# Expert 1's second weights issued behind the last attention step, and two late gathers side by side

## The chip, the cores and the metric

The kernel runs on one core of a Trainium2 chip. The metric is the device time of one execution in microseconds (us); the time before is the median of three runs.

## The reference

Attention over blocks of 64 positions for 8 batches of 8 heads (576 positions, 64 wide) gives 4608 rows of 512 numbers. A block of queries sees its own block of keys and all earlier ones. Each row is then sent to one of 8 experts, which its `domain_id` names:

```python
scores = np.where(mask, scale * q @ k.transpose(0, 1, 3, 2), -1e9)   # mask: block_i >= block_j
attn = softmax(scores); x = (attn @ v)                                # -> 4608 rows of 512
for e in range(8):
    rows = domain_id == e
    h = np.maximum(x[rows] @ w1[e], 0.0)      # w1[e]: 512 x 1024
    out[rows] = h @ w2[e]                     # w2[e]: 1024 x 512
```

The routing depends on `domain_id` alone. Each expert gets 640 slots (5 blocks of 128 rows); a loop at the end would serve an expert with more rows.

## The kernel before, in words

**Attention** runs in 33 steps (the loop at L535). Step p computes the scores of head pair p and the output of pair p - 1; a batch is four steps. The finished rows go to `x_rows`, a buffer in DRAM, by stores on SP's queue (`store_x`, L445): once per batch, and for the last batch in two pieces, 320 columns wide behind pair 30 and 192 columns wide behind pair 31. Each piece is two transfers (L448, L451).

**Experts.** For an expert the rows are gathered from `x_rows` into a tile `xg`, 128 rows at a time, transposed to `xT`, multiplied by w1 into `hT` (`mm1`, L650), by w2 into `po` (`mm2`, L663), and scattered to the output (L670). `xg` has four buffers, `xT` three. VectorE transposes a whole tile with 16 instructions (`turn`, L633); single blocks are transposed on TensorE and copied by VectorE (L482, L485).

The slots of each expert are filled so that its blocks 0 to 2 hold rows of batches 0 to 4 only. So these three blocks can be gathered while attention still runs on the last batches (`early_gather`, L499, which reads a shortened `x_rows`), and experts 0 and 1 begin with 384 columns each. Their blocks 3 and 4, and those of the others, need the last batch too: these gathers (`gather`, L468) wait for the last store. TensorE then goes through expert 0 blocks 0 to 2, expert 1 blocks 0 to 2, expert 0 blocks 3 and 4, expert 1 blocks 3 and 4, and after that experts 2 to 7 whole.

**What sets the order.** The schedule is written by hand: each engine executes what the program lists for it in that order. All loads of weights, all gathers and all scatters are issued by GpSimd (POOL) and go to one software DMA queue, q0; the stores of x go to SP's queue, q1. Both run on the same 16 DMA engines. POOL rotates over eight DMA semaphores (DMASW0 to DMASW7); before it issues a transfer it waits for the one that used the same semaphore eight transfers earlier.

Weights come in halves of 512 KB each: `load_weights` (L133) returns four functions, two halves of w1 and two of w2, and a list `todo` holds those still to be issued. The table `issue` (L528) says for each step what POOL issues behind it: a pair (e, w) is the early gather of expert e's block w, a 0 is the next half in `todo`. Behind the last step stand the remaining early gathers and then the late ones (L694 to L702).

Of the kernel before, what the change touches and what calls it, by code (L numbers as in the profile page):

```python
# [17 lines left out]
def kernel(  # L18
# [16 lines left out]
    NB = 5  # L35
# [5 lines left out]
    NE = 3  # L41
# [91 lines left out]
    def load_weights(w1_e, w2_e, pool=wsb, bufs=NW):  # L133
        w1h = pool.tile([128, 4, Fdim], F16, name="w1h", tag="w1h", bufs=bufs)
        w2h = pool.tile([128, 8, DM], F16, name="w2h", tag="w2h", bufs=bufs)
        return w1h, w2h, [lambda i=i: w1_half(w1h, w1_e, i) for i in range(2)] + [
            lambda i=i: w2_half(w2h, w2_e, i) for i in range(2)]
# [318 lines left out]
    def weights(e):  # L456
        where = (msb, 1) if e % (NW + 1) == NW else (wsb, NW)
        w1s[e], w2s[e], todo = load_weights(moe_w1[e], moe_w2[e], *where)
        return todo
# [6 lines left out]
    def gather(g, tok, blks):  # L466
        for blk in blks:
            nc.gpsimd.indirect_dma_start(  # L468
                out=g[:, blk, :], out_offset=None, in_=xd,
                in_offset=bass.IndirectOffsetOnAxis(  # L470
                    ap=tok[:, 1, blk : blk + 1], axis=0),
                bounds_check=N - 1, oob_is_err=False)

    def new_xg():
        return gsb.tile([128, NB, DM], F16, name="xg", tag="xg", bufs=4)

    def new_xT():
        return gsb.tile([128, 4, CAP], F16, name="xT", tag="xT", bufs=3)
# [18 lines left out]
    def early_gather(e, w):  # L497
        row = rows[e, w]
        nc.gpsimd.indirect_dma_start(  # L499
            out=xgs[e][:, w, :], out_offset=None, in_=xd[0 : N - LB * S],  # L500
            in_offset=bass.IndirectOffsetOnAxis(ap=row[:, 0:1], axis=0),
            bounds_check=N - LB * S - 1, oob_is_err=False)
# [17 lines left out]
    def turn_qk(*at):  # L520
        if at in Ts:
            G, s = Ts[at]
            if s == 0 and G > 1:
# [2 lines left out]

    prev = None
    issue = {22: (0, 0), 24: ((0, 0), 0), 25: ((0, 1), 0), 26: ((0, 2), 0),  # L528
             27: ((1, 0), 0), 28: ((1, 1), 0), 29: ((1, 2), 0), 30: ((2, 0),),
             31: ((2, 1),)}  # L530

    def tok_of(e):
        return tok0[:, :, NB * e : NB * e + NB]

    for p in range(npair + 1):  # L535
# [58 lines left out]
        if p == 22:  # L594
            todo = weights(0)
        if p == 24:
            todo += weights(1)
            xgs = [new_xg() for _ in range(4)]
# [42 lines left out]
    def new_hT():  # L641
        return msb.tile([128, 8, CAP], F16, name="hT", tag="hT", bufs=2)
# [49 lines left out]
        return outs[NB * e : NB * e + NB]  # L692

    early_gather(2, 2)  # L694
    for w in range(NE):
        early_gather(3, w)
    todo = weights(2)
    for e in range(3):
        for blk in range(NE, NB):
            gather(xgs[e], tok_of(e), (blk,))  # L700
            if e < 2 and blk == NE:
                todo.pop(0)()  # L702
    hT0, xT0, xT1, xT2 = new_hT(), xT, new_xT(), new_xT()
    turn(xgs[1], xT1, 0, NE)
    mm1(xT0, hT0, w1s[0], ((0, CE),))
# [2 lines left out]
    todo = weights(3)  # L708
# [28 lines left out]
    with tc.For_i(0, n_it, 1) as it:  # L737
# [5 lines left out]
        for _ in inv_high(msb, iv, NB, base_f[:, 0:1]):  # L743
# [7 lines left out]
        w1h, w2h, todo = load_weights(  # L751
            moe_w1[bass.ds(e_r, 1)].rearrange("o d f -> (o d) f"),
            moe_w2[bass.ds(e_r, 1)].rearrange("o d f -> (o d) f"))
# [38 lines left out]
```

## Time and profile before

| | us |
|---|---|
| median of 3 runs | 276.4 (272.78 to 277.53) |
| the profiled execution's own time | 274.43 |
| its span | 272.7 |
| TensorE busy (PE) | 252.2 (92%) |
| VectorE busy (DVE) | 186.8 (68%) |
| GpSimd busy (POOL) | 161.2 (59%) |
| mean granted TensorE clock | 0.975 |

Times in the rows below count from the start of the span. A wait in brackets is idle time of that engine just before the instruction, with what ended it. A POOL row of a transfer lasts as long as POOL writes its descriptors, not as long as the data move; the time from issue to landing is in the rows of the DMA view. An engine that is not busy costs nothing unless another waits for it.

### The profile page before, as it was taken

Reading aid. Unit: us, or ns where it says so; the run is one execution under the profiler, and the core shown is the slowest. Engines: PE = TensorE matmul, PEld = TensorE weight load, DVE = VectorE, ACT = ScalarE, POOL = GpSimd, SP = SyncE. Lnnn points to the kernel's source line nnn. Section 1 sums busy time; section 2 is a strip of 40 time slices with the busy share of each in tenths; the row PEclk is TensorE's granted clock in tenths of the full one; section 3 lists DMA queues with packets and bytes.
Section 4 is the critical chain, followed back from the end, with each engine's and each line's share of the span. In section 5 each row is a group of like instructions: output and inputs, shape, how many; then the busy total and the mean of one; then the engine's idle time right before and its main releaser. Section 6 shows DMA issues by size and latency. Waiting matters only on the chain.

```text
span 272.7 us, 7015 instructions
## 1 busy us (share of the span) xinstructions
PE 252.2 (92%) x2911; PEld 158.6 (58%) x2911; DVE 186.8 (68%) x303; ACT 164.9 (60%) x218; POOL 161.2 (59%) x189
## 2 busy tenths in 40 slices
PE   8999679999999999998799999999999999999940
PEld 5666456666666766663455665574655746647410
DVE  4589667999999787449149999079695893960000
ACT  1658667999999799953435655463553635536410
POOL 8798844644527156662888685477877876151240
PEclk9999977999999999999999999999999999999995
DMA  6999999999999999994889999999899996121130
GB/s 85 155 185 111 183 194 191 220 182 235 185 216 206 192 236 240 254 258 136 176 177 258 205 260 239 267 202 216 217 215 293 175 240 237 68 113 57 41 137 0
DMA packets 65665, 50.85 MB, mean 186 GB/s; under 512 B 41053, under 2 KB 53853, under 8 KB 65632
## 3 DMA queue, kind: packets, MB, share of 16 engines
q0 software_dynamic: 60016, 45.63, 98.0%
q1 hardware_dynamic: 5616, 4.76, 6.3%
q8 instruction: 24, 0.39, 0.5%
q14 instruction: 9, 0.07, 0.1%
HBM read 67.15 MB, written 15.20 MB: 302 GB/s over the span
## 4 chain that ended last, share of the span: by engine, by line
PE 57%; DMA 14%; issue 12%; POOL 10%; ACT 1%; POOLq 1%; DVE 0%; SPq 0%; ACTq 0%
PE ph L650 15%; PE po L663 14%; DMA kh<-in_k_dram 9%; PE ps L373 8%; PE po L415 8%; PE PT L362 6%; POOL out_dram L670 5%; PE po L426 4%; DMA xg<-x_rows,tok 4%; POOL vS L94 2%; DMA x_rows<-x 2%; PE ps L395 1%; POOL xg L468 1%; POOL qh L75 1%; ACT A L378 1%
## 5 line engine op out<-in xcount | busy, mean ns | idle before, releaser
L633 DVE STREAM_TRANSPOSE xT<-xg 32x640 f16<-32x640 f16 (+1 forms) x112 | 89.4, 798 | 22.8 <-DMA xg<-x_rows,tok 18.4
L378 ACT ACTIVATE A<-ps 128x1024 f16<-128x1024 f32 x96 | 92.0, 1024 | 16.7 <-PE ps L373 7.8
L650 PE MATMUL ph<-xT,w1h 128*128 128x320 f16 (+2 forms) x512 | 72.7, 299 | 3.1 <-DVE xT L633 2.8
L663 PE MATMUL po<-w2h,hT 128*128 128x512 f16 x320 | 71.0, 379 | 0.0
L654 ACT ACTIVATE hT<-ph 128x640 f16<-128x640 f32 (+2 forms) x80 | 47.8, 598 | 28.4 <-PE ph L650 26.3
L650 PEld LDWEIGHTS <-w1h 128*128 128x128 f16 x512 | 49.8, 98 | 25.9 <-issue 5.9
L670 POOL DMA_INDIRECT out_dram<-osb,tok x40 | 40.5, 1012 | 35.4 <-ACT osb L669 23.4
L663 PEld LDWEIGHTS <-hT 128*128 128x128 f16 x320 | 31.2, 98 | 35.5
L669 ACT COPY osb<-po 128x512 f32<-128x512 f32 x40 | 23.5, 586 | 46.6 <-PE po L663 42.1
L94 POOL DMA_DIRECT2D vS<-in_v_dram x45 | 36.2, 826 | 16.4 <-DMA kh<-in_k_dram 12.7
L365 DVE COPY QK<-PT 128x1152 f16<-128x1152 f16 x30 | 40.5, 1350 | 5.5 <-PE PT L362 5.5
L373 PE MATMUL ps<-QK 64*128 64x64 f16 (+3 forms) x320 | 40.2, 302 | 0.7 <-ACT A L378 0.6
L468 POOL DMA_INDIRECT xg<-x_rows,tok x28 | 28.4, 1014 | 15.6 <-issue 11.8
L415 PE MATMUL po<-vS,A 128*128 128x65 f16 x640 | 30.1, 198 | 0.4 <-DVE tf L225 0.3
L415 PEld LDWEIGHTS <-A 128*128 128x128 f16 x640 | 23.9, 100 | 9.7 <-issue 6.3
L439 DVE TENSOR_TENSOR x<-po,rc 128x640 f16<-128x640 f32 x32 | 26.4, 825 | 1.1
L499 POOL DMA_INDIRECT xg<-x_rows,row x12 | 12.6, 1048 | 15.5 <-DVE row L495 13.9
L426 PE MATMUL po<-vS,A 64*64 64x65 f16 (+1 forms) x320 | 21.2, 196 | 0.0
L373 PEld LDWEIGHTS <-QK 64*128 64x128 f16 x320 | 13.2, 95 | 6.1 <-issue 1.8
L426 PEld LDWEIGHTS <-A 64*64 64x64 f16 (+1 forms) x320 | 14.6, 108 | 1.9
L123 POOL DMA_DIRECT2D w1h<-in_moe_w_dram x16 | 12.2, 766 | 4.7 <-DMA qh<-in_q_dram 3.0
L438 DVE RECIPROCAL rc<-po 128x10 f32<-128x10 f32 x32 | 7.0, 220 | 10.5 <-PE po L426 9.7
(103 smaller groups left out, 142.4 us busy)
## 6 DMA issues: line engine op xcount, KB each, us to landing
w1h<-in_moe_w_dram POOLq DMA_DIRECT2D x16, 512.0 KB, 9.0
w2h<-in_moe_w_dram POOLq DMA_DIRECT2D x16, 512.0 KB, 9.5
x_rows<-x SPq DMA_DIRECT2D x7, 512.0 KB, 10.1
qh<-in_q_dram POOLq DMA_DIRECT2D x6, 576.0 KB, 13.1
kh<-in_k_dram POOLq DMA_DIRECT2D x6, 576.0 KB, 14.0
vS<-in_v_dram POOLq DMA_DIRECT2D x24, 128.0 KB, 11.8
vS<-in_v_dram POOLq DMA_DIRECT2D x23, 64.0 KB, 5.7
qh<-in_q_dram POOLq DMA_DIRECT2D x3, 288.0 KB, 6.7
```

The source lines that it names most:

```text
L94: nc.gpsimd.dma_start(out=vS[b % RV][r0:128, c, h0:h1, 16:80], in_=v[b, h0:h1, 128 * c : 128 * c + n, :].rearrange("h p d -> p h d"))
L365: nc.vector.tensor_copy(out=QKs[G][:, s].rearrange("p i (n j) -> p i n j", j=R), in_=P16.rearrange("p (j i n) -> p i n j", j=R, i=2))
L373: nc.tensor.matmul(out=o[:, t], lhsT=QK[h, 1, i, 128 * c : 128 * c + 128], rhs=QK[h, 0, i, q0:q1], start=True, stop=True)
L378: nc.scalar.activation(out=o, in_=i, func=AF.Exp, scale=0.125)
L415: nc.tensor.matmul(out=po[:, t, 65 * w : 65 * w + 65], lhsT=st["A"][:, t, n0 : n0 + 128], rhs=vS[b % RV][:, c, head(st, t), 15:80], start= ...
L426: nc.tensor.matmul(out=po[r0:128, t, 65 * w : 65 * w + 65], lhsT=st["A"][k : k + 64, t, n0 : n0 + 128 - r0], rhs=vS[b % RV][k : k + 64, c, ...
L468: nc.gpsimd.indirect_dma_start(out=g[:, blk, :], out_offset=None, in_=xd, in_offset=bass.IndirectOffsetOnAxis(ap=tok[:, 1, blk : blk + 1], ...
L633: nc.vector.transpose(out=dst[32 * j : 32 * j + 32, i, b0:b1], in_=src[32 * i : 32 * i + 32, j, b0:b1])
L650: nc.tensor.matmul(out=ph[:, i, 0:w], lhsT=w1_cols(w1h, dc, fc), rhs=xT[:, dc, c0 : c0 + w], start=(dc == 0), stop=(dc == 3))
L654: nc.scalar.activation(out=hT[:, fc, n0 : n0 + k * w].rearrange("p (i n) -> p i n", i=k), in_=ph[:, 0:k, 0:w], func=AF.Relu)
L663: nc.tensor.matmul(out=po[:], lhsT=hT[:, fc, 128 * blk : 128 * blk + 128], rhs=w2h[:, fc, :], start=(fc == 0), stop=(fc == 7))
L670: nc.gpsimd.indirect_dma_start(out=dst[blk], out_offset=bass.IndirectOffsetOnAxis(ap=tok[:, 0, blk : blk + 1], axis=0), in_=osb[:], in_off ...
```

## The change

The two halves of expert 1's w2 are no longer issued in steps 28 and 29 but behind the last step, after the gather of expert 3's block 0. Of the late gathers, the two of expert 0 now stand next to each other, as do those of expert 1 and of expert 2, with a half of expert 2's w1 between the pairs.

```diff
     issue = {22: (0, 0), 24: ((0, 0), 0), 25: ((0, 1), 0), 26: ((0, 2), 0),
-             27: ((1, 0), 0), 28: ((1, 1), 0), 29: ((1, 2), 0), 30: ((2, 0),),
+             27: ((1, 0), 0), 28: ((1, 1),), 29: ((1, 2),), 30: ((2, 0),),
              31: ((2, 1),)}
...
     early_gather(2, 2)
-    for w in range(NE):
+    early_gather(3, 0)
+    for f in todo:
+        f()
+    for w in range(1, NE):
         early_gather(3, w)
     todo = weights(2)
     for e in range(3):
-        for blk in range(NE, NB):
-            gather(xgs[e], tok_of(e), (blk,))
-            if e < 2 and blk == NE:
-                todo.pop(0)()
+        gather(xgs[e], tok_of(e), range(NE, NB))
+        if e < 2:
+            todo.pop(0)()
```

POOL from step 28 to the last early gather, before. `xg_2230` to `xg_2233` are the gathered rows of experts 0 to 3, `row11` is expert 1's block 1, `w2h_2229` is expert 1's w2:

```order
L499 DMA xg_2231<-x_rows,row11_2548 128x512 [waits DMASW1_49,DVE_49]
L128 DMA w2h_2229<-in_moe_w2_dram 128x2x1024 [waits DMASW2_49]
L499 DMA xg_2231<-x_rows,row12_2611 128x512 [waits DMASW3_49,DVE_49]
L128 DMA w2h_2229<-in_moe_w2_dram 128x2x1024 [waits DMASW4_49]
L499 DMA xg_2232<-x_rows,row20_2677 128x512 [waits DMASW5_49,DVE_49]
L499 DMA xg_2232<-x_rows,row21_2754 128x512 [waits DMASW6_49,DVE_49]
L499 DMA xg_2232<-x_rows,row22_2746 128x512 [waits DMASW7_49]
L499 DMA xg_2233<-x_rows,row30_2748 128x512 [waits DMASW0_49]
L499 DMA xg_2233<-x_rows,row31_2750 128x512 [waits DMASW1_49]
L499 DMA xg_2233<-x_rows,row32_2752 128x512 [waits DMASW2_49]
```

The same place in the changed kernel:

```order
L499 DMA xg_2231<-x_rows,row11_2548 128x512 [waits DMASW1_49,DVE_49]
L499 DMA xg_2231<-x_rows,row12_2610 128x512 [waits DMASW2_49,DVE_49]
L499 DMA xg_2232<-x_rows,row20_2675 128x512 [waits DMASW3_49,DVE_49]
L499 DMA xg_2232<-x_rows,row21_2752 128x512 [waits DMASW4_49,DVE_49]
L499 DMA xg_2232<-x_rows,row22_2744 128x512 [waits DMASW5_49]
L499 DMA xg_2233<-x_rows,row30_2746 128x512 [waits DMASW6_49]
L128 DMA w2h_2229<-in_moe_w2_dram 128x2x1024 [waits DMASW7_49]
L128 DMA w2h_2229<-in_moe_w2_dram 128x2x1024 [waits DMASW0_49]
L499 DMA xg_2233<-x_rows,row31_2748 128x512 [waits DMASW1_49]
L499 DMA xg_2233<-x_rows,row32_2750 128x512 [waits DMASW2_49]
```

Expert 1's blocks 1 and 2 (`row11`, `row12`) now follow each other, and both halves of its w2 stand behind six more gathers.

POOL right behind that, before (`w1h_2815` is expert 2's w1; the first of these gathers waits for all eight semaphores of SP's stores):

```order
L468 DMA xg_2230<-x_rows,tok0_145 128x512 [waits DMAHW4_49,DMAHW3_49,DMAHW5_49,DMAHW2_49,DMAHW6_49,DMAHW1_49,DMAHW7_49,DMAHW0_49,DMASW3_49]
L123 DMA w1h_2815<-in_moe_w1_dram 128x2x1024 [waits DMASW4_49]
L468 DMA xg_2230<-x_rows,tok0_145 128x512 [waits DMASW5_49]
L468 DMA xg_2231<-x_rows,tok0_145 128x512 [waits DMASW6_49]
L123 DMA w1h_2815<-in_moe_w1_dram 128x2x1024 [waits DMASW7_49]
L468 DMA xg_2231<-x_rows,tok0_145 128x512 [waits DMASW0_49]
L468 DMA xg_2232<-x_rows,tok0_145 128x512 [waits DMASW1_49]
L468 DMA xg_2232<-x_rows,tok0_145 128x512 [waits DMASW2_49]
```

The same place in the changed kernel:

```order
L468 DMA xg_2230<-x_rows,tok0_145 128x512 [waits DMAHW4_49,DMAHW3_49,DMAHW5_49,DMAHW2_49,DMAHW6_49,DMAHW1_49,DMAHW7_49,DMAHW0_49,DMASW3_49]
L468 DMA xg_2230<-x_rows,tok0_145 128x512 [waits DMASW4_49]
L123 DMA w1h_2815<-in_moe_w1_dram 128x2x1024 [waits DMASW5_49]
L468 DMA xg_2231<-x_rows,tok0_145 128x512 [waits DMASW6_49]
L468 DMA xg_2231<-x_rows,tok0_145 128x512 [waits DMASW7_49]
L123 DMA w1h_2815<-in_moe_w1_dram 128x2x1024 [waits DMASW0_49]
L468 DMA xg_2232<-x_rows,tok0_145 128x512 [waits DMASW1_49]
L468 DMA xg_2232<-x_rows,tok0_145 128x512 [waits DMASW2_49]
```

The second gathers of experts 0 and 1 each stand one place earlier, the two halves of w1 one place later. Behind these rows POOL's order is the same; on the other engines nothing has moved.

## Rows read from the trace of the kernel before

**Rows 1.** Timeline of PE, end of attention to expert 1: start us, us, line, operation.
```profile
117.44 5.65 PE L650 MATMUL ph<-xT,w1h 128*128 128x384 f16 x32
122.93 5.34 PE L663 MATMUL po<-w2h,hT 128*128 128x512 f16 x24
131.09 5.63 PE L650 MATMUL ph<-xT,w1h 128*128 128x384 f16 x32 [2.82 <-DVE xT L633]
136.56 0.61 PE L482 MATMUL po<-identh,xg 128*128 128x128 f16 x8
137.00 1.89 PE L663 MATMUL po<-w2h,hT 128*128 128x512 f16 x8
```

**Rows 2.** Timeline of DVE in the same stretch.
```profile
117.81 0.82 DVE L439 TENSOR_TENSOR x<-po,rc 128x640 f16<-128x640 f32 x1
121.63 9.31 DVE L633 STREAM_TRANSPOSE xT<-xg 32x384 f16<-32x384 f16 x16 [3.00 <-DMA xg<-x_rows,row]
```

**Rows 3.** Timeline of POOL, step 28 to the late gathers.
```profile
109.61 0.74 POOL L128 DMA_DIRECT2D w2h<-in_moe_w_dram  x1
110.65 1.07 POOL L499 DMA_INDIRECT xg<-x_rows,row  x1 [0.30 <-DMA xg<-x_rows,row]
119.78 1.00 POOL L499 DMA_INDIRECT xg<-x_rows,row  x1 [0.30 <-issue]
128.46 1.00 POOL L468 DMA_INDIRECT xg<-x_rows,tok  x1 [5.08 <-issue]
129.45 0.78 POOL L123 DMA_DIRECT2D w1h<-in_moe_w_dram  x1
```

**Rows 4.** DMA view, issues near 106.9, 110.7, 118.7, 119.1, 119.8, 128.5, 130.5: KB, us to landing.
```profile
w1h<-in_moe_w_dram POOLq DMA_DIRECT2D x1, 512.0 KB, 10.8
xg<-x_rows,row POOLq DMA_INDIRECT x1, 10.9
x_rows<-x SPq DMA_DIRECT2D x1, 192.0 KB, 8.7
x_rows<-x SPq DMA_DIRECT2D x1, 24.0 KB, 8.5
xg<-x_rows,row POOLq DMA_INDIRECT x1, 6.6
xg<-x_rows,tok POOLq DMA_INDIRECT x1, 2.8
xg<-x_rows,tok POOLq DMA_INDIRECT x1, 4.9
```

**Rows 5.** Windows: from:to us, engines' busy us, PE clock, DMA share, GB/s.
```profile
116.00:126.00 10.00, 9.93 (x79) 5.63 (x77) 6.18 (x17) 5.07 (x10) 5.02 (x5) 1.00 1.02 259
126.00:131.00 5.00, 2.27 (x11) 0.83 (x9) 4.84 (x9) 1.17 (x2) 2.24 (x3) 1.00 0.15 41
142.00:179.00 37.00, 36.69 (x233) 22.63 (x232) 28.14 (x43) 19.27 (x37) 24.41 (x27) 1.00 1.08 242
```

**Rows 6.** All loads of tile w2h: spread of the landing times.
```profile
DMA to landing us min/median/max: 6.5/9.5/14.8
```

**Rows 7.** Timelines of POOL, DVE, PEld and PE around experts 4 and 5.
```profile
157.14 1.01 POOL L670 DMA_INDIRECT out_dram<-osb,tok  x1 [1.64 <-ACT osb L669]
170.60 0.99 POOL L468 DMA_INDIRECT xg<-x_rows,tok  x1 [1.54 <-DMA w1h<-in_moe_w_dram]
178.78 13.58 DVE L633 STREAM_TRANSPOSE xT<-xg 32x640 f16<-32x640 f16 x16 [8.15 <-DMA xg<-x_rows,tok]
194.76 13.58 DVE L633 STREAM_TRANSPOSE xT<-xg 32x640 f16<-32x640 f16 x16 [2.40 <-DMA xg<-x_rows,tok]
192.47 2.57 PEld L650 LDWEIGHTS <-w1h 128*128 128x128 f16 x20 [0.35 <-issue]
192.51 8.85 PE L650 MATMUL ph<-xT,w1h 128*128 128x320 f16 x64
209.83 8.86 PE L650 MATMUL ph<-xT,w1h 128*128 128x320 f16 x64
```

## The prediction

> **What bounds the kernel now.** I read the timeline of TensorE first, from the end of attention to the last expert. From 117.4 us on it works without a break but for one gap: expert 0's second product ends at 122.93 + 5.34 = 128.27, and expert 1's first begins at 131.09, 2.82 us later, released by VectorE's transposes [rows 1]. From there matmuls follow each other to the end, so a microsecond closed in that gap is one off the total, if nothing later gives it back, and 2.82 us is all that there is to win. VectorE's timeline says why it is late: the 16 transposes of expert 1's rows take 9.31 us and begin at 121.63, though VectorE was done with attention at 117.81 + 0.82 = 118.63; for 3.00 us it waited for a gather [rows 2]. That gather is expert 1's block 2, which POOL issued at 110.65 between the two halves of w2 [rows 3]; it landed 10.9 us later, at 121.55, in a queue so full that the w1 half issued at 106.63 needed 10.8 and landed at 117.4 [rows 4].
>
> The DMA windows show the other side: the engines are saturated up to 126 (share 1.02, 259 GB/s), then nearly idle up to 131 (0.15, 41 GB/s) [rows 5]. In that hole POOL stands for 5.08 us before its first late gather [rows 3], which needs the last stores of x: issued at 118.66 and 119.06, landed after 8.7 and 8.5 us [rows 4], so at 127.4 and 127.6. The gather starts at 128.46, 0.9 us later.
>
> Then I looked for the next place where TensorE meets VectorE with nothing to spare. It is expert 4: its 16 transposes run from 178.78 to 178.78 + 13.58 = 192.36, TensorE starts on them at 192.51, and the load of its weights came 0.35 us late, which it does not at the other experts [rows 7]. Slack there is nil. Expert 5's transposes end at 194.76 + 13.58 = 208.34, 1.5 us before TensorE's 209.83 [rows 7].
>
> **Part 1: the weights leave steps 28 and 29.** Between the w1 half (117.4) and the gather (121.55) the queue carried block 1's gather, one w2 half and the gather itself: 128 + 512 + 128 KB in 4.15 us. Without the half a third of that is left, 1.4 us, so the gather lands at about 118.8. In steps 28 and 29 two POOL issues go, of 0.74 us each [rows 3]; nobody waits for POOL there. VectorE is free at 118.63, so the transposes run from about 118.9 to 128.2; TensorE started 0.15 us after their end (131.09 against 121.63 + 9.31 = 130.94), so it starts at 128.35. Gain at this place: **2.7 us** (bounds: 0 if the gather doesn't move, 2.82).
>
> **Part 2: the weights arrive elsewhere.** They are issued after expert 3's block 0, at 119.78 + 1.00 = 120.8 and, at 0.78 for the issue of a half [rows 3], at 121.6. TensorE wants them at 137.00 - 2.7 = 134.3 [rows 1]. Loads of w2 take 6.5 to 14.8 us, 9.5 in the middle [rows 6]: landing at 131.1, cover of 3 us; at the worst 136.4, a stall of 2.1 us that leaves the change 0.6 us ahead. I take nothing for it. The transfers fill the hole of rows 5. POOL itself gets longer there by two issues: 120.8 + 2 x 0.78, then two gathers with gaps of 0.30, so its first late gather can't start before 125.25. That is still before 128.46.
>
> **Part 3: when the last store lands.** This sets the late gathers, and through them all that POOL and the DMA queue do later. Before, it had the w2 halves and six gathers beside it. Now it has fewer bytes ahead and the w2 halves coming in beside its end. Bounds: a gather in an empty queue landed after 2.8 us [rows 4], which would be 121.5 and leave POOL's own 125.25 as the limit; and as late as before, 127.6. It can't be much later, since the bytes are the same and the engines drained by about 126.3: allow 1.4 us for idle time that opens earlier. By bytes: from 117.4 six gathers (768 KB) and the stores (360 + 216 KB) are 1.38 MB, 5.3 us at 259 GB/s, so 122.7; the weights can move from about 121.8 and take a share of the last 0.24 MB, which stretches it to 123.7 at equal shares, to 126.4 if they get four fifths; about 1.3 us until it is reported (2.8 less 1.0 of issue and 0.5 for 128 KB) gives 125.0 to 127.7. The nearest row is the gather issued at 119.78 into that same stretch, which landed 6.6 us later [rows 4]; the second store's 119.06 + 6.6 is **125.7**. I take that; the first late gather then starts at about 126.5, 2.0 us earlier than before (bounds: 3.2 earlier, 1.4 later).
>
> **Part 4: the late gathers.** Expert 0's second one no longer stands behind a w1 half. It was issued at 130.53 and landed after 4.9, at 135.4 [rows 4]; TensorE transposed it at 136.56 [rows 1]. With the gap closed TensorE comes at 133.85. Now it is issued 1.3 us behind the first, at 127.8, and with 2.8 to 4.9 us lands at 130.6 to 132.7: covered, and it would be by 0.4 us with a first gather at 128.46 and 2.8 us each way (132.6, or 134.7 with 4.9, 0.8 us late). Each w1 half moves back by one gather, 1.3 us; expert 2, which needs them, comes after both parts of experts 0 and 1. I cost this part at nothing; without it Part 1 would run into 135.4 and lose about 1.5 us.
>
> **Part 5: what follows.** From 128.46 [rows 3] to the wait at 157.14 [rows 7] POOL issues 24 transfers with gaps of no more than 0.31, and their count is the same after the change, so all moves by the same 2.0 us. At 157.14 it waits for a result of TensorE, which is 2.7 us earlier too [rows 7]. From 142 to 179 the DMA engines are saturated (1.08) [rows 5], and POOL stands for landings of weights eight transfers back, as at 170.60 [rows 7]; a saturated queue that begins 2.0 us earlier ends 2.0 us earlier. Expert 4's rows then land so that VectorE starts at 176.8 and ends at 190.4, TensorE starts at 190.5. It could have come at 192.51 - 2.7 = 189.8, so 0.7 us of Part 1 is given back. Expert 5's 1.5 us of slack and its own 2.0 us cover the rest.
>
> **Sum:** 2.7 - 0.7 = **2.0 us** less. The profiled execution took 274.43 (span 272.7 and 1.7 around it) and would take 272.4. The median shown, 276.4, lies 2.0 above it; the four times known (272.78, 274.43, 276.4, 277.53) have their middle at 275.4, and I put the forecast on that: **273.4**.
>
> **The rivals.** *Given back at expert 4*: the store lands at 127.6 as before, the gathers start as before, and TensorE finds expert 4's rows no earlier than 192.4. Gain 0.1, time 275.3. For it: the store still shares the engines with the same weights. Against: about 0.5 MB less stands ahead of it. Chance 0.22.
>
> *Slower, by the last store*: the weight halves, issued just when the second store is in progress, take so many turns that it lands at 129.0. Then POOL's first late gather is at 129.9, 1.4 us later than now, and expert 4's rows with it: 276.8. It decides at a landing past 127.6. For it: the store beside two weight halves needed 8.7 us, a gather in a drained queue 2.8. Against: before the weights begin, three us pass in which the store meets only gathers. Chance 0.13. The Trainium skill, page "DMA: Bandwidth & Descriptors", section "Queues, rings and completion order", says that each DMA engine takes turns between its queues by whole packets, of several descriptors each; by that the place behind the store protects it from nothing, and the sum would be this rival's. The trace before bears out the sharing, in the 8.5 to 8.7 us of small stores, but not the size of a turn.
>
> *All of it*: the store lands before 124.4, the gathers start at 125.25, and nothing is given back; 2.8 us, 272.6. Chance 0.15.
>
> *It does not do what it says*: the gather of block 2 is held by the stores rather than by the half ahead of it and lands past 120.5; the gap keeps 1.8 us or more; gain at most 1.0, 274.4. Against: 512 of the 768 KB in its stretch go. Chance 0.08.
>
> My forecast, a gain of 1 to 2.6 us, keeps 0.42.
>
> **The numbers.** The cases run from 272.6 to 276.8; the four times of one kernel scatter by 2.4 us to either side, and a median of several by perhaps 1.8. So the low end is 272.6 - 1.8 = 270.8, and the high end is 276.8, which the two worst cases reach only with a run above the middle. Two per cent, about what a measurement of this kernel tells from no change, is 5.5 us. No case wins or loses that: faster by more than 2% has 0.1 and slower 0.05, both by scatter or by something that I don't see, and 0.85 is for within 2%.
>
> **What would show it.** VectorE's wait of 3.00 us before expert 1's transposes is gone, and TensorE's of 2.82; POOL's first late gather starts near 126.5; the hole in the DMA windows after 126 is filled and lies earlier; expert 4's transposes start near 176.8, with a break of about 0.7 us on TensorE before expert 4. If the gap is closed and the span is not shorter, look at expert 4; if the first late gather is later than 128.46, the store is at fault.

## The result, and the profile after

The changed kernel took **271.9 us** (median of 20 runs, 270.18 to 273.99) beside 276.39 for the kernel before (20 runs, 272.78 to 277.96). The ratio is 0.9869, 95% interval [0.9841, 0.9898]: 3.6 us less (2.8 to 4.4). Executions more than 1.5% above the fastest of their kernel are left out of every ratio here, which is why this one is not the 0.984 of the medians, and the profiled executions of e1 and e6 below are of that sort. 273.4 was forecast, in a range of 270.8 to 276.8. The profiled execution took 271.8 us, its span is 270.1. In it attention ended 0.42 us later than in the profile before (first expert matmul at 117.86, before 117.44), so counted from there the experts got 3.0 us shorter: (272.7 - 117.44) - (270.1 - 117.86) = 3.02.

TensorE's timeline, end of attention to expert 1, answers to [rows 1]:

```profile
117.86 5.64 PE L650 MATMUL ph<-xT,w1h 128*128 128x384 f16 x32
123.34 5.34 PE L663 MATMUL po<-w2h,hT 128*128 128x512 f16 x24
128.52 5.63 PE L650 MATMUL ph<-xT,w1h 128*128 128x384 f16 x32
133.98 0.61 PE L482 MATMUL po<-identh,xg 128*128 128x128 f16 x8
134.43 1.89 PE L663 MATMUL po<-w2h,hT 128*128 128x512 f16 x8
```

The third row has no bracket any more: the gap of 2.82 us is gone. VectorE's timeline says why; it goes from attention straight into the transposes, where it stood for 3.00 us before [rows 2]:

```profile
118.22 0.82 DVE L439 TENSOR_TENSOR x<-po,rc 128x640 f16<-128x640 f32 x1
118.96 9.30 DVE L633 STREAM_TRANSPOSE xT<-xg 32x384 f16<-32x384 f16 x16
```

POOL's timeline, against [rows 3]: the two weight loads stand at 121.16, and the first late gather (L468) follows POOL's own work with 0.30 us between, so nothing of the stores holds it now.

```profile
120.15 1.01 POOL L499 DMA_INDIRECT xg<-x_rows,row  x1 [0.30 <-issue]
121.16 1.53 POOL L128 DMA_DIRECT2D w2h<-in_moe_w_dram  x2
122.99 1.07 POOL L499 DMA_INDIRECT xg<-x_rows,row  x1 [0.30 <-issue]
124.37 1.05 POOL L499 DMA_INDIRECT xg<-x_rows,row  x1 [0.30 <-issue]
125.72 1.00 POOL L468 DMA_INDIRECT xg<-x_rows,tok  x1 [0.30 <-issue]
```

The DMA view has the last stores (issued at 119.07 and 119.47), the gather at 120.15, the two weight halves and the second late gather, each with its us to landing, against [rows 4] and [rows 6]:

```profile
x_rows<-x SPq DMA_DIRECT2D x1, 192.0 KB, 3.1
x_rows<-x SPq DMA_DIRECT2D x1, 24.0 KB, 3.1
xg<-x_rows,row POOLq DMA_INDIRECT x1, 3.6
w2h<-in_moe_w_dram POOLq DMA_DIRECT2D x2, 512.0 KB, 7.9
xg<-x_rows,tok POOLq DMA_INDIRECT x1, 4.2
```

The last stores landed at 122.2 and 122.6, five us earlier than before (127.4 and 127.6). The windows, against [rows 5] (behind the busy times of the five engines come TensorE's clock, the DMA share and GB/s): the two parts of the old hole, full queue and empty queue, have evened out.

```profile
116.00:126.00 10.00, 9.92 (x83) 5.82 (x80) 9.12 (x23) 5.48 (x11) 6.94 (x8) 1.00 0.82 192
126.00:131.00 5.00, 5.00 (x28) 2.56 (x27) 2.23 (x4) 2.40 (x5) 4.09 (x5) 1.00 0.99 231
142.00:179.00 37.00, 36.77 (x234) 22.69 (x233) 28.82 (x44) 19.51 (x36) 25.14 (x28) 1.00 1.09 247
```

And experts 4 and 5, against [rows 7], from the timelines of POOL, VectorE and TensorE:

```profile
168.29 1.00 POOL L468 DMA_INDIRECT xg<-x_rows,tok  x1 [1.50 <-DMA w1h<-in_moe_w_dram]
175.54 13.58 DVE L633 STREAM_TRANSPOSE xT<-xg 32x640 f16<-32x640 f16 x16 [7.41 <-DMA xg<-x_rows,tok]
189.88 8.86 PE L650 MATMUL ph<-xT,w1h 128*128 128x320 f16 x64
192.60 13.58 DVE L633 STREAM_TRANSPOSE xT<-xg 32x640 f16<-32x640 f16 x16 [3.47 <-DMA xg<-x_rows,tok]
207.21 8.86 PE L650 MATMUL ph<-xT,w1h 128*128 128x320 f16 x64
```

Expert 4's transposes end at 189.12, TensorE comes at 189.88: 0.76 us of slack where 0.7 us of loss was expected.

### The profile page after: what moved, and what is told of

Same layout as the page of the kernel before. It is cut to its first block, busy times and chain, and to the rows that moved or that the text cites. A ratio compares the mean times of both kernels' runs of the same rounds, so it can differ in the third digit from the quotient of the medians.

```text
span 270.1 us, 7016 instructions
## 1 busy us (share of the span) xinstructions
PE 251.7 (93%) x2911; PEld 158.6 (59%) x2911; DVE 187.6 (69%) x303; ACT 164.8 (61%) x218; POOL 161.4 (60%) x189
## 4 chain that ended last, share of the span: by engine, by line
PE 64%; issue 11%; DMA 10%; POOL 9%; ACT 1%; DVE 1%; POOLq 1%
PE ph L650 21%; PE po L663 19%; PE ps L373 7%; PE po L415 7%; DMA kh<-in_k_dram 5%; PE PT L362 5%; POOL out_dram L670 4%; PE po L426 3%; DMA qh<-in_q_dram 3%; DMA xg<-x_rows,row 2%; POOL vS L94 2%; PE ps L395 1%; POOL xg L499 1%; POOL w1h L123 1%; PE po L220 1%
## 5 line engine op out<-in xcount | busy, mean ns | idle before, releaser
L654 ACT ACTIVATE hT<-ph 128x640 f16<-128x640 f32 (+2 forms) x80 | 47.8, 597 | 25.4 <-PE ph L650 25.0
L468 POOL DMA_INDIRECT xg<-x_rows,tok x28 | 28.5, 1018 | 11.2 <-issue 6.7
L362 PE MATMUL PT<-identh,qh 128*64 128x128 f16 x270 | 10.9, 228 | 4.5 <-DMA qh<-in_q_dram 4.3
```

The lines of the kernel that those rows point to most:

```text
L468: nc.gpsimd.indirect_dma_start(out=g[:, blk, :], out_offset=None, in_=xd, in_offset=bass.IndirectOffsetOnAxis(ap=tok[:, 1, blk : blk + 1], ...
L654: nc.scalar.activation(out=hT[:, fc, n0 : n0 + k * w].rearrange("p (i n) -> p i n", i=k), in_=ph[:, 0:k, 0:w], func=AF.Relu)
```

## The experiments

Ratios are to the kernel before, run on the same chip. The diffs are against the changed kernel, unless another is named. What the trace of one execution says beside it: "experts" is the span less the start of the first expert matmul, "stops" are TensorE's idle times after that, "late" is where the first late gather starts. For e1 and e6 the table gives the ratio alone; what their traces add is said where it bears on a reading.

| run | ratio, 95% interval | experts | stops, with the place | late |
|---|---|---|---|---|
| before | | 155.3 | 2.82 before expert 1 | 128.46 |
| change | 0.9869 [0.9841, 0.9898] | 152.2 | none | 125.72 |
| e0 before, again | 1.0020 [0.9966, 1.0074] | 155.9 | 0.40 in expert 0, 0.88 before 1, 1.46 in 4, 0.35 in 6 | 128.08 |
| e1 weights only | 0.9906 [0.9852, 0.9959] | | | |
| e2 gathers only | 0.9970 [0.9909, 1.0031] | 156.5 | 0.37 in 0, 1.74 before 1, 0.27 before 4, 0.89 in 6 | 129.07 |
| e3 beside the store | 1.0027 [0.9965, 1.0090] | 162.3 | 1.04 before 1, 1.03 before 0's block 3, 1.58 before 4, 3.83 in 6 | 128.50 |
| e4 change, again | 0.9910 [0.9871, 0.9950] | 152.8 | 0.34 in 0 | 124.84 |
| e5 change, 18 osb | 0.9891 [0.9838, 0.9944] | 157.2 | 0.36 in 0, 2.74 in 6 | 125.58 |
| e6 before, 18 osb | 0.9979 [0.9927, 1.0030] | | | |
| e7 one half ahead | 0.9896 [0.9818, 0.9975] | 156.5 | 0.40 before 4, 0.79 in 4, 0.22 in 5, 1.59 in 6 | 125.80 |
| e8 no load | 0.9986 [0.9932, 1.0041] | 155.8 | 2.80 in 0 | 123.37 |
| e9 behind the late ones | 0.9936 [0.9884, 0.9989] | 155.2 | 1.68 in 0, 0.26 before 0's block 3, 0.47 in 4 | 123.69 |
| e10 change, a third time | 0.9861 [0.9795, 0.9927] | 152.9 | 0.50 in 6 | 126.43 |
| e11 small loads | 0.9889 [0.9801, 0.9976] | 153.6 | 0.58 before 1, 0.44 in 4 | 124.98 |

**e0 and e4, both kernels again.** No edit.

> The kernel before, unchanged, for a second profile. The ratio should be 1.00 within 0.3%. The changed kernel's medians differ by 4.5 us and its profile by 2.6 us only. Theory A (the first profile of before, 274.43 us, was of a short execution; a typical one, near 276.4, has longer stalls at the same two places): TensorE's gap before expert 1 or a stall at expert 4 is longer than in the first profile by up to 2 us. Rival B (the rest is spread over the start of attention, where loads are waited for): the gap stays at 2.8 us and the time before step 2 of attention differs instead.

> The changed kernel, unchanged, beside the variants and on their chip. Theory A (the gap of 2.8 us before expert 1 is closed, and the late gathers and with them the DMA queue of experts 2 to 7 start 2.7 to 3.2 us earlier): ratio to before 0.984 to 0.991, last store landed within 4 us of its issue, first late gather at POOL's own limit, 6.7 us behind the last store's issue. Rival B (on a chip where transfers take longer the queue is the bound from expert 4 on whatever is done here): ratio 0.993 to 1.000 although the gap is closed.

The unchanged kernel against itself gives 1.002: a difference of half a per cent can be noise here. The change keeps its gain. TensorE's timeline of e0 shows something that the first trace did not (the rows are from expert 0's second product, expert 1 and expert 4):

```profile
126.21 3.84 PE L663 MATMUL po<-w2h,hT 128*128 128x512 f16 x17 [0.40 <-ACT hT L654]
130.93 5.63 PE L650 MATMUL ph<-xT,w1h 128*128 128x384 f16 x32 [0.88 <-DVE xT L633]
...
196.08 6.68 PE L650 MATMUL ph<-xT,w1h 128*128 128x320 f16 x48 [1.46 <-ACT hT L654]
```

The gap before expert 1 is 0.88 us in this execution, and 2.2 us are lost in other places, in stops where TensorE waits for ScalarE's relu (`hT`, L654) inside an expert. The sum, 3.1 us, is near the 2.82 of the first trace. One execution of the kernel before is thus not all of them; its gap is 2.82 us in one and 0.88 in the other.

**e1 and e2, the two parts of the change by themselves.** e1 has the weights behind the last step but the late gathers of one expert apart, as before; e2 is the kernel before with the late gathers side by side.

```diff
 e1
-        gather(xgs[e], tok_of(e), range(NE, NB))
-        if e < 2:
-            todo.pop(0)()
+        for blk in range(NE, NB):
+            gather(xgs[e], tok_of(e), (blk,))
+            if e < 2 and blk == NE:
+                todo.pop(0)()
 e2, against the kernel before: these lines the other way round
```

> Only the weights are moved behind the last step; the late gathers are split by the w1 halves as before. Theory A (everything comes from the place of the weights: with the store landing near 122 and the late gathers starting at 125.7, expert 0's second gather stands behind a w1 half and still lands at 125.7 + 2.1 + 4.9 = 132.7, before TensorE wants it at 134): same time as the changed kernel, ratio 0.985 to 0.990. Rival B (the pairing is needed, as the prediction's Part 4 had it for late stores): expert 0's second gather lands after 134 and TensorE waits 0.5 to 1.5 us before expert 1's second product; ratio 0.991 to 0.995.

> Only the late gathers are paired; the weights stay in steps 28 and 29. Theory A: the gap before expert 1 stays at 2.8 us, expert 4's transposes end no earlier, ratio 0.998 to 1.002. Rival B (the pairing itself brings something, since expert 0's and 1's rows land 1.3 us earlier): ratio 0.993 to 0.997.

The weights alone bring 0.9906, and the interval lies below 1; the gathers alone bring nothing that can be told from 1. So the place of the weights is enough for a gain. Whether the pairing adds a few tenths on top is not decided: the interval of e1 covers both theories.

The trace of e1 shows that the gap itself does not measure what the weights cost. In it the gap before expert 1 is as long as in the kernel before:

```profile
128.87 5.63 PE L650 MATMUL ph<-xT,w1h 128*128 128x384 f16 x32 [2.62 <-DVE xT L633]
```

But attention ended 2 us earlier there (first expert matmul at 115.43); VectorE waited for expert 1's block 2 and began its transposes at 119.41. Counted from the start of each span, they begin at 121.63, 121.47 and 122.34 in before, e0 and e2, where the weights stand in steps 28 and 29, and between 118.59 and 119.69 in every run that moved them (in e6, the kernel before with more output buffers, at 120.23). The gap is what is left between that landing and the end of attention, which wanders (first expert matmul from 115.4 to 118.7). Expert 1's first matmul starts at 131.09, 130.93 and 131.80 in the three executions with the old place, and at 128.52, 128.17 and 129.25 in the three of the change (after, e4, e10): some 2.6 us earlier. In e6 it starts at 129.81, with no gap before it.

**e3, the weights beside the last store.** Issued in steps 30 and 31, so still behind expert 1's gathers, but ahead of the store.

```diff
-             27: ((1, 0), 0), 28: ((1, 1),), 29: ((1, 2),), 30: ((2, 0),),
-             31: ((2, 1),)}
+             27: ((1, 0), 0), 28: ((1, 1),), 29: ((1, 2),), 30: ((2, 0), 0),
+             31: ((2, 1), 0)}
...
-    early_gather(3, 0)
-    for f in todo:
-        f()
-    for w in range(1, NE):
+    for w in range(NE):
```

> The weights are issued in steps 30 and 31, behind the gathers of expert 2's blocks 0 and 1: behind expert 1's last early gather, but ahead of the last store of x; late gathers paired. Theory A (two places have to be opened: the gap before expert 1, and the landing of the last store, which sets the late gathers and through the saturated queue expert 4's rows): the gap is closed, but the store lands at 125 to 127.5 beside the weights, the first late gather starts at 126 to 128.4, and expert 4 gives back what is missing to 125.7; ratio 0.990 to 0.999. Rival B (only the place of the weights behind expert 1's last early gather counts): ratio 0.985 to 0.989, as the changed kernel, and no stall at expert 4.

The whole gain is gone (1.0027). The DMA view has the two last stores, issued at 117.79 and 118.20; then POOL's first late gather, and TensorE at expert 1, at expert 0's block 3, and at expert 4:

```profile
x_rows<-x SPq DMA_DIRECT2D x1, 192.0 KB, 9.6
x_rows<-x SPq DMA_DIRECT2D x1, 24.0 KB, 9.4
```
```profile
128.50 1.00 POOL L468 DMA_INDIRECT xg<-x_rows,tok  x1 [5.14 <-issue]
```
```profile
128.44 5.63 PE L650 MATMUL ph<-xT,w1h 128*128 128x384 f16 x32 [1.04 <-DVE xT L633]
137.27 0.40 PE L482 MATMUL po<-identh,xg 128*128 128x128 f16 x4 [1.03 <-DMA xg<-x_rows,tok]
192.87 8.85 PE L650 MATMUL ph<-xT,w1h 128*128 128x320 f16 x64 [1.58 <-issue]
```

The store needs 9.4 us instead of 3.1, and the late gather stands 5.14 us for it. TensorE waits 1.04 us before expert 1, where attention again ended early (116.58), and on top of that for late rows: 1.03 us at expert 0's block 3, 1.58 at expert 4, whose transposes end at 192.72. Theory A has the mechanism; the loss is larger than its 0.990 to 0.999. The longest stops of this execution, 3.83 us in expert 6, stand behind late relus of ScalarE, whose cause is open, so the store explains 2.6 of the 7.5 us in the table. So it is not enough that the weights leave the way of expert 1's gathers; they must leave the way of the store as well.

**e7, one half ahead of the store.** The first half in step 30, the second where the change has both.

```diff
-             27: ((1, 0), 0), 28: ((1, 1),), 29: ((1, 2),), 30: ((2, 0),),
+             27: ((1, 0), 0), 28: ((1, 1),), 29: ((1, 2),), 30: ((2, 0), 0),
```

> The changed kernel with the first of the two halves issued in step 30, ahead of the last store, the second behind expert 3's block 0 as in the change. Theory A (each half that stands in the queue ahead of the last store costs its landing about 3 us: 3.1 us with none, 9.6 with both): the store lands 5.5 to 7.0 us after its issue, which is at or just past POOL's own limit of 6.7 less 0.9; first late gather no more than 1.3 us later than in the change, ratio no more than 0.004 above it. Rival B (any weights beside the store cost the whole): lands after 8 us or more, first late gather 2.5 us later than in the change, ratio 0.998 to 1.003.

POOL's timeline at the first late gather:

```profile
123.26 1.00 POOL L499 DMA_INDIRECT xg<-x_rows,row  x1 [0.30 <-issue]
125.80 1.00 POOL L468 DMA_INDIRECT xg<-x_rows,tok  x1 [1.54 <-issue]
```

It waits 1.54 us. The record of this store's landing is missing; if the gather starts 0.9 us behind it, as in the kernel before and in e3, the store (second piece issued at 119.10) landed after some 5.8 us. With 3.1 for none (2.9 to 4.0 in e4, e5, e10 and e11) and 9.4 for two, each half that is issued ahead of the store costs it about 3 us. Of these 2.7 us POOL's own order hides 1.5 (it could not have come before 123.26 + 1.00 + 0.30 = 124.56); of the 1.2 us left over the trace shows 0.40 as a stop before expert 4, and the ratio nothing (0.9896, with a wide interval).

**e5 and e6, more output buffers.** The stops inside experts 4 and 6 might have come from ScalarE waiting for a free `osb` tile, whose scatters go through the full queue. e5 is the change, e6 the kernel before, each with this edit:

```diff
-            osb = msb.tile([128, DM], F32, name="osb", tag="osb", bufs=10)
+            osb = msb.tile([128, DM], F32, name="osb", tag="osb", bufs=18)
```

> The changed kernel with 18 instead of 10 buffers for the result rows (osb). Theory A (the stalls inside experts 4 and 6 of the kernel before come from ScalarE, which waits for a buffer whose scatter has not landed, and behind it stands the relu that TensorE waits for): with 18 no such stall is left, ratio to before 0.005 or more below that of the changed kernel here, if its own execution shows such stalls; no difference if it has none. Rival B (those stalls come from late gathers or late weights): no difference, within 0.003.

> The kernel before with 18 instead of 10 buffers for the result rows. Theory A: the stalls of 1.5 and 0.4 us inside experts 4 and 6 are gone, ratio 0.992 to 0.996; the gap before expert 1 stays. Rival B: ratio 0.998 to 1.002, stalls stay.

Neither ratio moves. e5's profiled execution even has the longest such stop: 2.74 us inside expert 6, behind a relu before which ScalarE stood idle for 2.38 us, for no cause that the trace names. More buffers do not remove these stops.

**e8, e9 and e11, the late gathers earlier.** Without the two weight loads ahead of it, POOL could start the late gathers two us sooner. e8 removes the loads and lets expert 1 multiply by expert 0's second weights (the loading of its own is left out); e9 puts the loads behind expert 0's two late gathers.

```diff
 e8
-    for f in todo:
-        f()
+    w2s[1] = w2s[0]
 e9
-    for f in todo:
-        f()
+    w2_1 = todo
...
         gather(xgs[e], tok_of(e), range(NE, NB))
+        if e == 0:
+            for f in w2_1:
+                f()
```

> The changed kernel without the two loads of expert 1's w2: expert 1 multiplies by expert 0's w2 instead, so 1 MB less is moved and POOL issues two transfers less ahead of the late gathers. Theory A (in the change these loads stand in a hole of the DMA engines and are hidden; TensorE has no gap left to win): the same time as the changed kernel run beside it, within 0.004 of its ratio. Rival B (the DMA queue of experts 2 to 7 is what ends last, so that each load costs its transfer): 0.008 to 0.015 below it, 2 to 4 us.

> The changed kernel with the two halves one place further back: behind the two late gathers of expert 0. The first late gather can then start about 2 us earlier (at 123 to 124 instead of 125.7), the halves are issued at about 125.5 and 126.3. Theory A (POOL's list of issues sets what follows, and the count up to expert 4 is the same): the same time as the changed kernel within 0.004; the halves land at 132 to 134, just before TensorE wants them at 134.1, a stall of at most 0.5 us. Rival B (the transfers of the DMA engines set it: the hole from 116 to 124 is longer by 2 us and comes back as a stall at expert 4): 0.005 to 0.008 above it.

> The changed kernel, unchanged, beside these two. Ratio to before 0.987 to 0.991, where the two comparisons so far overlap; a gain of 3.0 us, as between the two first profiles once their starts are set equal, would be 0.989.

e10 is the change beside them, 0.9861. Both theories on e8 fell: with a megabyte less to load it is 1.3% slower than the change. e9 is 0.0075 above the change, which is what its rival B had forecast, but the two intervals overlap and its stop is in expert 0, not at expert 4. TensorE's timeline of e8 in expert 0, ScalarE's last three relus of that expert, and POOL's first late gather:

```profile
123.15 0.81 PE L650 MATMUL ph<-xT,w1h 128*128 128x384 f16 x4 [0.64 <-ACT hT L654]
123.80 1.67 PE L663 MATMUL po<-w2h,hT 128*128 128x512 f16 x7
127.45 3.84 PE L663 MATMUL po<-w2h,hT 128*128 128x512 f16 x17 [1.98 <-issue]
```
```profile
122.61 0.49 ACT L654 ACTIVATE hT<-ph 128x384 f16<-128x384 f32 x1 [0.96 <-PE ph L650]
124.08 0.49 ACT L654 ACTIVATE hT<-ph 128x384 f16<-128x384 f32 x1 [0.98 <-PE ph L650]
126.91 0.49 ACT L654 ACTIVATE hT<-ph 128x384 f16<-128x384 f32 x1 [2.33 <-remote]
```
```profile
123.37 1.00 POOL L468 DMA_INDIRECT xg<-x_rows,tok  x1 [0.30 <-issue]
```

The late gathers did start early, at 123.37, and nobody needed them so soon; but ScalarE stood idle for 2.33 us before the last relu, where it is 0.16 in the change's trace ("remote": the trace names no instruction of this core that released it), and TensorE stood for it before the eighth matmul of the second product. e9 has the same stop at the same matmul, 1.68 us. Both have a hole in the DMA engines' work just there (share 0.41 and 0.38 from 122 to 128, 1.00 in the change). e11 keeps the hole and takes the early start away: two loads of 32 KB in the place of the two halves.

```diff
-    for f in todo:
-        f()
+    for i in range(2):
+        nc.gpsimd.dma_start(
+            out=w2s[1][:, 4 * i : 4 * i + 2, 0:64].rearrange("p (c r) f -> p c r f", r=2),
+            in_=moe_w2[1][512 * i : 512 * i + 256, 0:64].rearrange(
+                "(c p r) f -> p c r f", p=128, r=2))
+    w2s[1] = w2s[0]
```

> The change with the two 512 KB loads of expert 1's second weights replaced by two loads of 64 columns each (32 KB), at the same place in POOL's order; expert 1 multiplies by expert 0's second weights instead, so the loading of its own is left out. POOL issues as many instructions as in the change, so its first late gather can start at about 125.5 as there, and not at 123.4 as when the loads were removed altogether; but the queue has 0.94 MB less to move between 121 and 129, so the hole in the DMA engines' work is there as it was then. Theory A (the hole itself makes ScalarE's last relus of expert 0 late): ratio 0.995 to 1.000, a relu of expert 0 that starts 1.5 to 2.5 us late, and a stop of 1.5 to 2.5 us in expert 0's second product. Rival B (what made them late is that the late gathers began at 123.4, two microseconds earlier): ratio 0.985 to 0.991, as the change; first late gather at 125.3 to 126, and no stop of over 0.7 us in expert 0.

The same window (122 to 128 us) of e8 and then of e11, DMA share and GB/s last, and TensorE in expert 0 of e11:

```profile
122.00:128.00 6.00, 3.38 (x18) 1.48 (x16) 5.76 (x11) 1.47 (x3) 4.80 (x5) 1.00 0.41 96
```
```profile
122.00:128.00 6.00, 6.00 (x30) 2.64 (x27) 5.85 (x12) 2.15 (x4) 4.83 (x5) 1.00 0.41 78
```
```profile
122.67 5.34 PE L663 MATMUL po<-w2h,hT 128*128 128x512 f16 x24
128.59 5.63 PE L650 MATMUL ph<-xT,w1h 128*128 128x384 f16 x32 [0.58 <-DVE xT L633]
```

The DMA share is 0.41 in both, but TensorE is busy for 6.00 us in e11 and for 3.38 in e8. So an empty queue by itself does not make the relu late; theory A fell, on one execution. What rival B forecast came true, a ratio like the change's (0.9889) and no stop in expert 0. Counted from the first expert matmul, the late gathers began after 6.2 us in e8 and 6.3 in e9, and after 7.8 or more in all the others, of which none in the table stopped for more than 0.4 us in expert 0 before its late blocks.

But the traces speak against its reason. In e8 ScalarE stood idle for 0.96 us before the relu at 122.61, ahead of the first late gather at 123.37, and 0.82 of TensorE's 2.80 us lie before that gather too; in e9 ScalarE's first long idle time, 1.37 us, ends at 123.53, and the gather begins at 123.69. And e6's execution stops for 1.01 us in expert 0 although its late gathers begin 9.2 us behind the first expert matmul. What delays ScalarE stays open, and one execution of each kernel is traced.

## Why the prediction was right

The forecast lay within 0.6% of the measured time, and Parts 1 and 2 held; one term was mis-sized, in Part 3, to the change's disadvantage, and the loss of Part 5 fell with it. That the time came so near is in part luck: the forecast stands on 275.4 for the kernel before, 1.0 us below the median that was measured beside the change (276.39), and this made up for part of a gain that was put 1.0 to 1.6 us too low.

- **Part 1 was right.** 2.7 us were forecast at the gap; expert 1's first matmul starts 10.66 us behind expert 0's first instead of 13.65, 2.99 us. VectorE starts its transposes at 118.96; 118.9 was forecast. e1 shows that moving the weights, and with it Parts 1 to 3, carries the gain. That 2.82 us was all there was to win holds for the first trace alone: the gap depends on when attention ends, as e0 and e1 show.
- **Part 2 was right.** The halves land 7.9 us after their issues, by about 130, in time for 134.43. The limit of POOL for the first late gather, 125.25 by the sum, was 125.72 with the 0.42 us of the later start.
- **Part 3 is the step that was mis-sized.** I took 6.6 us for the last store, from a gather that had met a full queue; it took 3.1, near the lower bound. The sum by bytes, which seemed to support the 6.6, had six gathers still to be moved from 117.4 on. Six gathers do stand ahead of the weights in POOL's order (which puts the two halves five and four gathers further back than before, not six). But POOL had issued three of them by 113.98, two more at 117.54 and 118.85, and the last only at 120.15, behind the store's second piece (119.47). From 117.54 on it issues a gather every 1.3 us, which for 128 KB is about 100 GB/s, less than the 259 by which the sum went. Once the weights are out of steps 28 and 29 the queue is not full from 118 on:

```profile
118.00:120.00 2.00, 2.00 (x13) 1.16 (x12) 1.95 (x4) 0.98 (x2) 1.54 (x2) 1.00 0.64 193
120.00:122.00 2.00, 2.00 (x13) 1.08 (x12) 1.95 (x5) 1.47 (x3) 1.85 (x3) 1.00 0.78 198
122.00:124.00 2.00, 2.00 (x13) 1.08 (x12) 1.96 (x4) 1.44 (x3) 1.70 (x2) 1.00 0.76 113
```

 So the store landed at 122.6 and not at 125.7, and POOL by itself became the limit of the late gathers. That is the rival *all of it*, to which I had given 0.15. The rule of the Trainium skill (page "DMA: Bandwidth & Descriptors", section "Queues, rings and completion order"), that each engine takes turns between its queues by packets, is not put to the test by the change: the store was done at 122.6, when the second half had just been issued, so the two hardly met. Where they do meet, in e3, the store waits 9.4 us; the size of a turn is not shown there either. The rival *slower, by the last store* names the right danger, and e3 is the place where it happens.
- **Part 4 was not needed.** The second late gather landed at 127.03 + 4.2 = 131.2, 2.8 us before TensorE transposed its rows (133.98). The store's early landing gave that cover; the 1.5 us of loss that I named for a change without the pairing supposed a first gather at 128.46. e1 gives 0.9906 without it, not to be told from the change.
- **Part 5 was right in its mechanism, and its 0.7 us fell with Part 3.** The first late gather moved by 3.2 us counted from the start of the experts (128.46 - 117.44 against 125.72 - 117.86), not by 2.0, and the gather at 170.60 before, 168.29 after, by 2.7. Expert 4's rows came 3.7 us earlier by the same count, and the slack there is 0.76 us; why they gained one us more than their gather did is not shown. e7 bears the mechanism out: its first late gather begins 0.45 us later than the change's by this count, and TensorE stops for 0.40 us before expert 4.
- **The level.** 2.0 us of gain and a middle of 275.4 gave 273.4. The gain was 3.0 in the pair of profiles, 3.6 (2.8 to 4.4) in the first comparison, and 0.991 and 0.9861 in the two repeats. Part of what is more in the runs than in the sum may be the stops of 0.3 to 1.5 us in experts 4 and 6 that e0 and e2 have and the change's three traces have but once (0.50 in e10). That the change removes them is not shown: e5, the change with more buffers, has one of 2.74. The prediction had no such term, since the first trace of before did not show them.

## What to carry to other kernels

A large transfer that is wanted late should not be issued ahead of a small one that others wait for: here a half of 512 KB held the gather behind it for up to 3 us, two of them ahead of the store held that for 6, and only behind both did the gain stay. Before adding up what stands ahead of a transfer, look at when each piece was issued: a queue fed every 1.3 us with 128 KB is not a full queue. And read more than one execution before saying that a gap is all there is to win; the same kernel lost its 3 us in one place in one execution and in four places in another. Where a transfer and an engine meet, compare when each comes, not the gap between them: the gap also closes when the engine is late.

## What was not expected of the hardware

**Taking work away made it slower.** e8 moves a megabyte less than the change and issues its gathers earlier, and is 1.3% slower (five executions against four); in its trace TensorE stops for 2.80 us in expert 0, for relus that came late. The idle queue alone does not do it (e11), and the late gathers cannot have begun it by starting earlier, since the first relus are late before them. Stops at a late relu stand inside experts 4 and 6 of several executions of both kernels, too, and more output buffers leave them (e5, e6). What they are stays open. One rival no run tests: in every trace a queue that the profile calls `q14 instruction` moves a little between 115 and 123 us and between 226 and 233, in experts 0 and 6, where most of these stops stand; but in the change's trace it does so without a stop, and near the stops in expert 4 it moves nothing.

**A stop of 2.7 us can cost more than itself.** In e5 TensorE is idle from 227.2 to 229.9 in expert 6, and then its granted clock falls. The row, and the windows behind it:

```profile
229.91 8.35 PE L650 MATMUL ph<-xT,w1h 128*128 128x320 f16 x48 [2.74 <-issue]
```
```profile
230.00:231.00 1.00, 1.00 (x6) 0.56 (x6) 0.99 (x2) 0.43 (x1) 0.00 (x0) 0.60 0.49 185
231.00:232.00 1.00, 1.00 (x5) 0.55 (x4) 0.99 (x2) 0.28 (x1) 0.00 (x0) 0.50 0.00 0
232.00:233.00 1.00, 1.00 (x5) 0.59 (x4) 0.99 (x2) 0.70 (x1) 0.00 (x0) 0.50 0.00 0
233.00:234.00 1.00, 1.00 (x7) 0.59 (x5) 0.97 (x3) 0.04 (x1) 0.00 (x0) 0.70 0.00 0
```

The clock is 0.50, the lower of the two levels (1.2 of 2.4 GHz), for some three us. These 48 matmuls took 8.35 us where 6.68 is the rule (e0's row above), 1.67 us on top of the 2.74. The clock falls in the same way behind the stops of 4.21, 3.40 and 3.35 us in expert 6 of e1, e3 and e6. The gap of 2.82 us in the kernel before, as long as e5's stop, was followed by 32 matmuls in 5.63 us [rows 1], at full clock: the length of the stop alone does not decide it.
